# q and k of batches 1 to 3 loaded in 32-column halves and transposed by VectorE in 32x32 blocks

## The chip, the cores and the metric

The kernel runs on one core of a Trainium2 chip. TensorE (PE) multiplies matrices and writes PSUM, VectorE (DVE) and ScalarE (ACT) do elementwise work, GpSimd (POOL) does casts and issues DMAs, SyncE (SP) issues DMAs; each engine works through its own instructions in order, and semaphores tie them together. Sixteen DMA engines move the data. The metric is the device time in microseconds (us); lower is better.

## The reference

Attention in which a query only sees keys of the same hash bucket, then a gated feed-forward block on its output. Four batches, 8 heads, 768 tokens, 64 columns a head; so 3072 tokens of width 512, and an inner width of 1536.

```python
q_bits = (einsum('bhsd,dk->bhsk', q, proj) > 0)        # 6 bits
k_bits = (einsum('bhsd,dk->bhsk', k, proj) > 0)
mask = q_bucket[:, :, :, None] == k_bucket[:, :, None, :]
scores = where(mask, q @ k.T / 8, -1e9)
attn = softmax(scores) @ v                              # per batch and head
x = attn, heads side by side                            # [3072, 512]
g, val = x @ w_gate, x @ w_val                          # [3072, 1536]
ffn_out = (gelu(g) * val) @ w_out
out = x + sigmoid(x @ w_res) * ffn_out
```

## The kernel before

The work is cut into 16 pairs of heads, pair n being heads 2j and 2j+1 of batch b, n = 4b + j.

*Loading.* `load_pair(n)` (lines 75 to 81) fetches q, k and v of a pair as float32 tiles qs, ks, vs of 128 partitions by 2 heads by 6 by 64. Partition p holds tokens 6p to 6p+5, so one run in DRAM is 6 x 64 x 4 = 1536 B. Each of the three tiles has three buffers, so the load of pair n waits until pair n-3 has been read. Pairs 0 and 1 are issued on SP and ACT, all others on POOL, which also issues the weights (lines 140 to 151).

*Preparing.* `prep_pair(n)` (line 160) makes the pair's operand `aug`, 71 rows by 1536 columns for each head: 64 rows of q and k transposed and scaled (columns 0 to 767 q, 768 to 1535 k), and 7 rows of sign bits, by which the matmul of scores gives equal buckets a large bonus. It is a generator; each call of next() emits one step:
- steps 1 to 3: four PE transposes of 128x128 float32 each into a PSUM tile `tps` (line 170), and a copy to `trT` by ACT (line 174) or, for the second group of pairs from 2 on, by DVE (line 172);
- step 4: eight hash matmuls into two PSUM tiles `hps` (line 195), the signs `bits` by DVE (line 180), four small DMAs on SP that put them into rows 64 to 70 of `aug` (line 185), and the first half of the scaled copy to `aug` by DVE (line 187);
- step 5: the second half of that copy.

The tiles tps, hps and those of the feed-forward (gps, vps, rps, ops) take turns in the same three PSUM buffers (`mm_psum`).

*The main loop* (line 386) has 192 steps, 24 (`LB`) for each half batch of queries and 6 for each pair in it. A step emits two score matmuls (`sc`, line 238) and their exponential on ACT (`e`, line 241), then, two steps behind, six matmuls of attention times v (`av`, line 258), then a step of a preparation if one is due, then pieces of the feed-forward of the previous half batch: `vps` (value matmuls, line 300, with the product `gh` on DVE, line 303), `rps` and `ops` (lines 308 and 315, with `y` and `o` on DVE and the output DMA on SP, line 323). How many pieces a step gets is set by a fixed rate, not by time. At the end of a half batch x is transposed (`xps`) and the gate matmuls (`gps`, line 290) run in a row. The table `begin` says at which step the preparation of a pair starts: pairs 4 to 7 at steps 30, 36, 42 and 48, later ones every 12 steps. Loads are emitted at begin - 14.

`TS` (line 40) is the order of the 128-token tiles, even ones first, which follows from how two tiles share one transpose.

Of the kernel before, what the change touches and what calls it, by code (L numbers as in the profile page):

```python
# [13 lines left out]
ALU = mybir.AluOpType  # L14
# [5 lines left out]
def kernel(  # L20
# [19 lines left out]
    TS = [t for par in range(2) for t in range(par, T, 2)]  # L40
# [41 lines left out]


# [26 lines left out]
    ind = const.tile([P, 2], FP32, name="ind")  # L110
    for side in range(2):
        nc.vector.tensor_reduce(
            ind[:, side:side + 1],
            ident.rearrange("p (h s c) -> p h s c", h=2, s=2)[:, :, side, NBITS:NR],
            axis=AX.XY, op=ALU.add)
    shift = const.tile([P, 1], FP32, name="shift")
    nc.vector.tensor_scalar(shift, ind[:, 0:1], -1.5, 0.5, op0=ALU.mult, op1=ALU.add)
    nc.vector.scalar_tensor_tensor(shift, ind[:, 1:2], 0.25 * NBITS - 0.5, shift,
                                   op0=ALU.mult, op1=ALU.add)
# [40 lines left out]
    def prep_pair(n):  # L160
# [18 lines left out]
        for par in range(2):  # L179
            nc.vector.tensor_scalar(bits[:, par, :], hp[par][:, 0:CH], 0.0, shift,  # L180
                                    op0=ALU.is_gt, op1=ALU.subtract)
# [4 lines left out]
        for par in range(2):  # L186
            nc.vector.tensor_scalar_mul(  # L187
                a[0:D].rearrange("d h (s p n) -> d (h s) p n", s=2, p=2)[:, :, par, :],
                trT[par * D:(par + 1) * D, :].rearrange("d (i n) -> d i n", i=4), QKS)
            yield par == 0  # L190
    def hash_bits(hp, trT, groups):
# [6 lines left out]
    def prep_first():  # L198
# [13 lines left out]
        for hh in range(2):  # L212
# [4 lines left out]
            for side in range(2):  # L217
                row = 32 * (2 * hh + side)
                nc.vector.tensor_scalar(
                    a[D:KAUG, hh, side * S:(side + 1) * S].rearrange("r (p n) -> r p n", p=2),  # L220
                    hp[row:row + NR, :, 0:CH], 0.0, shift[row:row + NR], op0=ALU.is_gt, op1=ALU.subtract)
# [22 lines left out]
    def attend(i):  # L244
# [9 lines left out]
        for x in range(2):  # L254
            jt = 2 * jp + x
            for t in range(TC):
                o = (hh * TC + t) * DV
                nc.tensor.matmul(av[:, o:o + D + 1], e[:, x, t * P:(t + 1) * P],  # L258
                                 va[:, 2 * j + hh, TS[jt], :],
# [34 lines left out]
    def feed_forward(u):  # L294
# [10 lines left out]
        for t in range(TC):  # L305
# [8 lines left out]
            for kk in range(KF):  # L314
# [7 lines left out]
            nc.vector.scalar_tensor_tensor(o, y, 0.5, x_tok[u][:, t, :], op0=ALU.mult, op1=ALU.add)  # L322
            nc.sync.dma_start(
                out[b * S:(b + 1) * S, :].rearrange("(p t) d -> p t d", t=T)[:, TS[c * TC + t], :], o)
# [47 lines left out]
    def prepare(i):  # L372

        nonlocal prep
        if prep is None and todo and i >= begin[todo[0]]:
# [5 lines left out]
            prep = prep_pair(n)  # L381
# [4 lines left out]
    for i in range(NS + LEAD):  # L386
# [7 lines left out]
        for n in loads.pop(i, []):  # L394
            load_pair(n, nc.gpsimd)
# [53 lines left out]
```

## Time and profile before

| what | value |
|---|---|
| three timed runs | 376.73 us median (376.04 to 379.93) |
| the profiled execution | 378.85 us, of which the span is 377.0 |
| PE / DVE / ACT / POOL busy | 362.9 / 172.1 / 255.7 / 54.7 us |
| PE transposes (tps, L170), 180 instructions | 36.7 us busy, 5% of the chain |
| PE clock granted | 0.8 to 0.9 of full speed in the first 60 us, then full |
| DMA | 31.56 MB, engines 75 to 112% busy until 60 us, 6 to 37% after |

Busy times of lines overlap, since matmuls are pipelined: what an instruction adds to PE's time is its share of the chain, or the distance of its start from the next one's. In the chain each piece is followed back from the last instruction to what released it. "Idle before, releaser" in a group of instructions says what its engine waited for.

### The profile page before, as it was taken

The page shows a single profiled execution, that of the slowest core. Times are in us where ns is not written, and L with a number is a line of the kernel's source. Part 1 is how long each engine was busy: PE and PEld are TensorE (multiplying, and loading weights), DVE is VectorE, ACT ScalarE, POOL GpSimd, SP SyncE. Part 2 cuts the span into 40 slices and gives each one's busy share as a digit, 9 for nine tenths or more (in the row PEclk, how much of TensorE's full clock was granted, in tenths as well). Part 3 has the DMA queues.
Part 4 walks back from the last instruction along what each step waited for, and adds up shares of the span by engine and source line. Part 5 has one row for each costly group of instructions (what it writes and reads, how often), then busy time and mean ns, then how long its engine had stood idle before and what let it go on. Part 6 is the DMA issues. An engine that isn't in the chain of part 4 may idle for free.

```text
span 377.0 us, 7850 instructions
## 1 busy us (share of the span) xinstructions
PE 362.9 (96%) x3215; PEld 222.7 (59%) x3238; DVE 172.1 (46%) x305; ACT 255.7 (68%) x373; POOL 54.7 (15%) x77
## 2 busy tenths in 40 slices
PE   8788999999999999999999999999999999999995
PEld 4455666665665656665666656756566556655652
DVE  3664115667275362554346352553625242534252
ACT  5568787666866768676786768766687778686410
POOL 0973312330033200303003100000000000000000
PEclk9788699999999999999999999999999999999999
DMA  7799960444033140124103010000100010000002
GB/s 246 239 222 210 257 278 24 144 142 164 7 130 132 46 169 2 41 98 150 61 1 130 31 34 28 2 6 29 63 2 0 30 50 7 2 30 29 30 1 83
DMA packets 14140, 31.56 MB, mean 84 GB/s; under 512 B 1972, under 2 KB 6648, under 8 KB 14104
## 3 DMA queue, kind: packets, MB, share of 16 engines
q0 software_dynamic: 7984, 21.76, 20.4%
q1 hardware_dynamic: 5816, 9.10, 6.7%
q8 instruction: 25, 0.41, 0.4%
q10 hardware_dynamic: 304, 0.20, 0.2%
q14 instruction: 11, 0.09, 0.1%
HBM read 29.36 MB, written 6.29 MB: 95 GB/s over the span
## 4 chain that ended last, share of the span: by engine, by line
PE 89%; issue 3%; DVE 3%; DMA 3%; ACT 1%; POOL 0%; SPq 0%; POOLq 0%; DVEq 0%; ACTq 0%
PE gps L290 17%; PE ops L315 16%; PE vps L300 16%; PE sc L238 16%; PE av L258 9%; PE rps L308 5%; PE tps L170 5%; PE hps L195 4%; PE xps L280 2%; DMA ks<-in_k_dram 1%; DMA aug<-bits 1%; DVE aug L187 1%; DVE bits L180 1%; ACT e L241 0%; DVE gh L303 0%
## 5 line engine op out<-in xcount | busy, mean ns | idle before, releaser
L241 ACT ACTIVATE e<-sc 128x768 bf16<-128x768 f32 x192 | 152.6, 811 | 66.5 <-PE sc L238 65.5
L238 PE MATMUL sc<-aug 71*128 71x384 bf16 x384 | 96.3, 335 | 2.3 <-ACT trT L174 0.8
L303 DVE TENSOR_TENSOR gh<-vps,gh 128x384 bf16<-128x384 f32 x96 | 52.7, 555 | 91.2 <-PE vps L300 70.3
L300 PE MATMUL vps<-xT,wv 128*128 128x384 bf16 x384 | 75.2, 326 | 0.0
L258 PEld LDWEIGHTS <-e 128*128 128x128 bf16 x1152 | 58.2, 100 | 25.9 <-issue 5.3
L315 PE MATMUL ops<-wo,gh 128*128 128x512 bf16 x282 | 70.5, 379 | 0.8 <-issue 0.8
L258 PE MATMUL av<-vaug,e 128*128 128x65 bf16 x1152 | 63.4, 197 | 1.7 <-DVE xtok L268 1.7
L290 PE MATMUL gps<-xT,wg 128*128 128x384 bf16 x384 | 64.3, 326 | 0.4 <-ACT xT L283 0.4
L238 PEld LDWEIGHTS <-aug 71*128 71x128 bf16 x384 | 36.9, 100 | 33.4 <-issue 4.6
L290 PEld LDWEIGHTS <-wg 128*128 128x128 bf16 x384 | 37.6, 98 | 26.6 <-issue 0.9
L292 ACT ACTIVATE gh<-gps 128x384 bf16<-128x384 f32 x96 | 45.4, 491 | 11.3 <-PE gps L290 10.2
L300 PEld LDWEIGHTS <-wv 128*128 128x128 bf16 x384 | 34.0, 98 | 20.0 <-issue 3.7
L315 PEld LDWEIGHTS <-gh 128*128 128x128 bf16 x288 | 25.4, 98 | 24.3 <-issue 3.1
L320 DVE SCALAR_TENSOR_TENSOR y<-th,ops 128x512 f32<-128x512 bf16 x24 | 16.4, 685 | 43.6 <-PE ops L315 39.2
L187 DVE TENSOR_SCALAR aug<-trT 64x1536 bf16<-64x1536 f32 x30 | 30.0, 1000 | 0.4
L80 POOL DMA_DIRECT2D qs<-in_q_dram x14 | 10.3, 734 | 131.8 <-PE tps L170 126.4
L180 DVE TENSOR_SCALAR bits<-hps,shift 128x384 bf16<-128x384 f32 x30 | 17.1, 613 | 26.5 <-PE hps L195 26.5
L311 ACT ACTIVATE th<-rps 128x512 bf16<-128x512 f32 x24 | 14.3, 597 | 17.4 <-PE rps L308 17.4
L308 PE MATMUL rps<-wr,xT 128*128 128x512 bf16 x79 | 22.4, 379 | 1.0
L174 ACT COPY trT<-tps 128x512 f32<-128x512 f32 x31 | 17.8, 582 | 2.5 <-PE tps L170 2.5
L170 PE MATMUL tps<-ident,qs 128*128 128x128 f32 x90 | 18.5, 290 | 0.7 <-DMA qs<-in_q_dram 0.7
L170 PE MATMUL tps<-ident,ks 128*128 128x128 f32 x90 | 18.2, 287 | 0.9 <-DMA ks<-in_k_dram 0.9
(48 smaller groups left out, 211.8 us busy)
## 6 DMA issues: line engine op xcount, KB each, us to landing
out_dram<-o SPq DMA_DIRECT2D x24, 256.0 KB
qs<-in_q_dram POOLq DMA_DIRECT2D x14, 384.0 KB, 3.5
ks<-in_k_dram POOLq DMA_DIRECT2D x14, 384.0 KB, 4.7
vs<-in_v_dram POOLq DMA_DIRECT2D x14, 384.0 KB, 5.3
wg<-in_moe_w_gate_dram POOLq DMA_DIRECT2D x4, 384.0 KB, 8.2
wv<-in_moe_w_val_dram POOLq DMA_DIRECT2D x4, 384.0 KB, 12.8
wo<-in_moe_w_out_dram POOLq DMA_DIRECT2D x4, 384.0 KB, 15.6
aug<-bits SPq DMA_DIRECT2D x60, 10.5 KB
```

The lines of the kernel that those rows point to most:

```text
L170: nc.tensor.transpose(ps[:, i * P:(i + 1) * P], tiles[4 * g + i], ident)
L180: nc.vector.tensor_scalar(bits[:, par, :], hp[par][:, 0:CH], 0.0, shift, op0=ALU.is_gt, op1=ALU.subtract)
L187: nc.vector.tensor_scalar_mul(a[0:D].rearrange("d h (s p n) -> d (h s) p n", s=2, p=2)[:, :, par, :], trT[par * D:(par + 1) * D, :].rearra ...
L238: nc.tensor.matmul(sp[:, x, 0:CH], a[:, S + jt * P:S + (jt + 1) * P], a[:, c * CH:(c + 1) * CH], start=True, stop=True)
L241: nc.scalar.activation(e, sp[:, :, 0:CH], AF.Exp, scale=EXPS)
L258: nc.tensor.matmul(av[:, o:o + D + 1], e[:, x, t * P:(t + 1) * P], va[:, 2 * j + hh, TS[jt], :], start=(first and x == 0 and t == 0), stop ...
L290: nc.tensor.matmul(ps[:, 0:CH], wg[:, kk, m * P:(m + 1) * P], xT[u][:, kk, :], start=(kk == 0), stop=(kk == KM - 1))
L292: nc.scalar.activation(gh[u][:, m, :], ps[:, 0:CH], AF.Gelu)
L300: nc.tensor.matmul(ps[:, 0:CH], wv[:, kk, m * P:(m + 1) * P], xT[u][:, kk, :], start=(kk == 0), stop=(kk == KM - 1))
L303: nc.vector.tensor_mul(sl, ps[:, 0:CH], sl)
L308: nc.tensor.matmul(rps, xT[u][:, kk, t * P:(t + 1) * P], wr[:, kk, :], start=(kk == 0), stop=(kk == KM - 1))
L315: nc.tensor.matmul(ops, gh[u][:, kk, t * P:(t + 1) * P], wo[:, kk, :], start=(kk == 0), stop=(kk == KF - 1))
```

## The change

For batches 1 to 3 (pairs 4 to 15) loading and preparing are written anew; pairs 0 to 3 stay.

`load_blocks(n)` brings q and k in a layout in which transposing 32x32 blocks is all that is needed. Token 32m + p goes to partition p of a quadrant of 32 partitions; the quadrant is chosen by head and by half of the 64 columns. One tile takes four DMAs of 32 partitions by 24 by 32 float32, and a run in DRAM is 32 x 4 = 128 B. v comes with token 128t + p on partition p, in runs of 256 B. All nine DMAs of a pair are issued on SP in place of POOL.

`prep_blocks(n)` transposes with two DVE instructions, one for q and one for k, each 128 by 768 float32 from SBUF to SBUF. The result has head hh on partitions 64hh to 64hh+63. Steps: 1 transpose of q, 2 transpose of k, 3 hash matmuls, signs and their DMAs, 4 and 5 the scaled copies, one a head. The sign constant has other signs per row now, and so a second one is made at the start. Token order is natural in batches 1 to 3, which changes `TS` and the addresses of the output rows there.

```diff
+    def load_blocks(n):
+        b, j = pairs[n]
+        for nm, src in (("q", q), ("k", k)):
+            s = stage.tile([P, S // Q, Q], FP32, tag=nm + "s", name=nm + "s")
+            for hh in range(2):
+                for c in range(D // Q):
+                    g = hh * D + c * Q
+                    nc.sync.dma_start(
+                        s[g:g + Q],
+                        src[b, 2 * j + hh, :, c * Q:(c + 1) * Q].rearrange("(m p) d -> p m d", p=Q))
+            staged[(nm, n)] = s
+        s = stage.tile([P, 2, T, D], FP32, tag="vs", name="vs")
+        nc.sync.dma_start(s, v[b, 2 * j:2 * j + 2].rearrange("h (t p) d -> p h t d", p=P))
+        staged[("v", n)] = s
...
+    def prep_blocks(n):
+        b, j = pairs[n]
+        trT = tr_pool.tile([P, 2, S], FP32, tag="trT", name="trT")
+        for side, nm in enumerate("qk"):
+            nc.vector.transpose(trT[:, side, :], staged.pop((nm, n)).rearrange("p m d -> p (m d)"))
+            yield True
+        hp = [mm_psum.tile([P, 512], FP32, tag="mm", name="hps") for _ in range(2)]
+        for i in range(4):
+            for hh in range(2):
+                nc.tensor.matmul(hp[hh][32 * i:32 * i + 32, 0:CH], proj_pair[hh * D:(hh + 1) * D, :],
+                                 trT[hh * D:(hh + 1) * D, i // 2, (i % 2) * CH:(i % 2 + 1) * CH],
+                                 start=True, stop=True)
+        bits = s_pool.tile([P, 2, CH], BF16, tag="bits", name="bits")
+        for hh in range(2):
+            nc.vector.tensor_scalar(bits[:, hh, :], hp[hh][:, 0:CH], 0.0, shifts[1],
+                                    op0=ALU.is_gt, op1=ALU.subtract)
+        a = aug_of(b, j)
+        for i in range(4):
+            nc.sync.dma_start(a[D:KAUG, :, i * CH:(i + 1) * CH], bits[32 * i:32 * i + NR])
+        yield True
+        for hh in range(2):
+            nc.vector.tensor_scalar_mul(a[0:D, hh, :], trT[hh * D:(hh + 1) * D].rearrange("d s n -> d (s n)"), QKS)
+            yield hh == 0
...
-            prep = prep_pair(n)
+            prep = prep_pair(n) if n <= 3 else prep_blocks(n)
...
-            load_pair(n, nc.gpsimd)
+            load_blocks(n)
```

On DVE, the preparation of pair 4 stands among the feed-forward products `gh` of the first half batch (aug_134 before and aug_140 now is the operand of pair 4; rec and xtok belong to the attention). Before:

```order
L267 RECIPROCAL rec<-av 128x6
L268 TENSOR_TENSOR xtok<-av,rec 128x2x3x64
L303 TENSOR_TENSOR gh<-vps,gh 128x384
L172 COPY trT<-tps 128x512
L303 TENSOR_TENSOR gh<-vps,gh 128x384 x2
L180 TENSOR_SCALAR bits<-hps,shift 128x384 x2
L187 TENSOR_SCALAR aug_134<-trT 64x4x384
L303 TENSOR_TENSOR gh<-vps,gh 128x384
L187 TENSOR_SCALAR aug_134<-trT 64x4x384
```

And now:

```order
L314 RECIPROCAL rec<-av 128x6
L315 TENSOR_TENSOR xtok<-av,rec 128x2x3x64
L218 STREAM_TRANSPOSE trT<-qs 128x768
L350 TENSOR_TENSOR gh<-vps,gh 128x384
L218 STREAM_TRANSPOSE trT<-ks 128x768
L350 TENSOR_TENSOR gh<-vps,gh 128x384
L228 TENSOR_SCALAR bits<-hps,shift_131 128x384 x2
L350 TENSOR_TENSOR gh<-vps,gh 128x384
L235 TENSOR_SCALAR aug_140<-trT 64x1536
L350 TENSOR_TENSOR gh<-vps,gh 128x384
L235 TENSOR_SCALAR aug_140<-trT 64x1536
```

One copy from PSUM is gone and two transposes from the loaded tiles have come, each ahead of a product; the bits stand one step earlier, and a product lies between them and the first scaled copy.

On SP, the queue held only the bits and the outputs once the first pairs were loaded. Before, from the bits of pair 3 (aug3) to the bits of pair 6:

```order
L185 DMA aug3_133<-bits_422 7x768 x4
L185 DMA aug4_134<-bits_921 7x768 x4
L185 DMA aug5_135<-bits_1060 7x768 x4
L323 DMA out_0_dram<-o_1090 128x512
L185 DMA aug6_136<-bits_1204 7x768 x4
```

And now, from the bits of pair 3 to the bits of pair 4 (the next rows are the load of pair 7, the bits of pair 5, an output, the load of pair 8):

```order
L207 DMA aug3_139<-bits_428 7x768 x4
L93 DMA qs_518<-in_q_dram 32x24x32 x4
L93 DMA ks_523<-in_k_dram 32x24x32 x4
L98 DMA vs_528<-in_v_dram 128x12x64
L93 DMA qs_600<-in_q_dram 32x24x32 x4
L93 DMA ks_605<-in_k_dram 32x24x32 x4
L98 DMA vs_610<-in_v_dram 128x12x64
L93 DMA qs_790<-in_q_dram 32x24x32 x4
L93 DMA ks_795<-in_k_dram 32x24x32 x4
L98 DMA vs_800<-in_v_dram 128x12x64
L232 DMA aug4_140<-bits_906 7x2x384 x4
```

The loads of pairs 4, 5 and 6 stand in a row between the bits of pair 3 and those of pair 4. On POOL the same loads stood behind the weights.

35 lines of the change are left out of this document (20 added, 15 removed).

## The prediction

> **What bounds the kernel now.** I read the page first (busy shares, then the chain), then the busy time by windows, then the chain in order of time around one prepared pair, then the groups by line, and last the DMA queues and the issue times. The page's busy line and chain, and two windows of 40 us from the middle of the run (the second column is PE):
>
> ```profile
> span 377.0 us, 7850 instructions
> PE 362.9 (96%) x3215; PEld 222.7 (59%) x3238; DVE 172.1 (46%) x305; ACT 255.7 (68%) x373; POOL 54.7 (15%) x77
> ...
> PE 89%; issue 3%; DVE 3%; DMA 3%; ACT 1%; POOL 0%; SPq 0%; POOLq 0%; DVEq 0%; ACTq 0%
> PE gps L290 17%; PE ops L315 16%; PE vps L300 16%; PE sc L238 16%; PE av L258 9%; PE rps L308 5%; PE tps L170 5%; PE hps L195 4%; PE xps L280 2%; DMA ks<-in_k_dram 1%; DMA aug<-bits 1%; DVE aug L187 1%; DVE bits L180 1%; ACT e L241 0%; DVE gh L303 0%
> ```
>
> ```profile
> 100.00:140.00 40.00, 39.74 (x391) 24.81 (x393) 24.32 (x42) 27.61 (x39) 9.02 (x12) 1.00 0.32 107
> 220.00:260.00 40.00, 39.90 (x363) 25.05 (x363) 19.96 (x36) 29.44 (x43) 0.00 (x0) 1.00 0.07 23
> ```
>
> PE is the bound, and in the middle it is so without a gap: 39.74 and 39.90 of 40 us. A busy PE need not be a PE at its peak, but the chain agrees: 89% of the span is PE following PE. So whatever leaves PE's queue there shortens the run by its pitch, as long as nothing that takes its place comes late. DVE (24.32 and 19.96 of 40) and ACT (27.61 and 29.44) have room. The transposes of this change (tps, L170) hold 5% of the chain.
>
> **What leaves PE.** Their pitch is read from the chain in order of time, not from the 270 ns that one lasts, because they overlap. Pair 9's preparation (start us, us, what):
>
> ```profile
> 152.38 0.65 PE vps L300 x4
> 153.03 0.33 PE sc L238 x2
> 153.36 0.44 PE tps L170 x4
> 153.80 0.65 PE vps L300 x4
> ...
> 155.14 0.47 PE tps L170 x4
> 155.61 0.65 PE vps L300 x4
> 156.26 0.33 PE sc L238 x2
> 156.59 0.19 PE av L258 x6
> 156.78 0.47 PE tps L170 x4
> 157.24 0.65 PE vps L300 x4
> 157.89 0.33 PE sc L238 x2
> 158.22 0.18 PE av L258 x6
> 158.40 0.81 PE hps L195 x16
> ```
>
> One pair gives PE 0.44 + 0.47 + 0.47 = 1.38 us of transposes. Pairs 4 to 15 lose them, 12 x 1.38 = **16.6 us**. (Check: 5% of 377.0 us for all 15 pairs of L170 is 18.9 us; twelve fifteenths of it are 15.1.) The hash matmuls (hps) stay, in the same number and shape. Pairs 0 to 3 keep the old way.
>
> **What DVE and ACT lose and get.** The groups concerned:
>
> ```profile
> L187 DVE TENSOR_SCALAR aug<-trT 64x1536 bf16<-64x1536 f32 x30 | 30.0, 1000 | 0.4
> L180 DVE TENSOR_SCALAR bits<-hps,shift 128x384 bf16<-128x384 f32 x30 | 17.1, 613 | 26.5 <-PE hps L195 26.5
> L303 DVE TENSOR_TENSOR gh<-vps,gh 128x384 bf16<-128x384 f32 x96 | 52.7, 555 | 91.2 <-PE vps L300 70.3 <-ACT e L241 14.5 <-ACT trT L174 4.7
> L322 DVE SCALAR_TENSOR_TENSOR o<-y,xtok 128x512 f32<-128x512 f32 x24 | 16.6, 692 | 0.8
> L172 DVE COPY trT<-tps 128x512 f32<-128x512 f32 x14 | 9.7, 691 | 15.7 <-PE tps L170 15.6
> L174 ACT COPY trT<-tps 128x512 f32<-128x512 f32 x31 | 17.8, 582 | 2.5 <-PE tps L170 2.5
> L241 ACT ACTIVATE e<-sc 128x768 bf16<-128x768 f32 x192 | 152.6, 811 | 66.5 <-PE sc L238 65.5
> ```
>
> ACT loses 24 copies of L174, 24 x 0.582 = 14.0 us; nothing waits for ACT on the chain beyond 1%, so this is worth nothing by itself. DVE loses 12 copies of L172, 8.3 us. It gets 24 block transposes of 128x768 float32, which no row shows. From 384 to 512 elements DVE's time goes from 555 (L303) to 692 ns (L322), 1.07 ns an element; 768 elements come to 692 + 256 x 1.07 = **966 ns**. From below the bound is 691 ns (the 512-element copy), from above 1.93 us (966 doubled, if four-byte blocks went at half that pace). I take 966, since both rows move 32-bit data or read it at one element a time. 24 x 0.966 = 23.2 us, net 23.2 - 8.3 = +14.9 us, DVE 172.1 to 187 us: still half of the span.
>
> Whether this reaches PE is decided where DVE is fullest, in the stretches where each step also has a vps group whose product (L303) DVE must take before its PSUM buffer, one of three, is free. There a step of PE is 0.65 + 0.33 + 0.19 = 1.17 us, and a pair's five steps with the hash 5 x 1.17 + 0.81 = 6.7 us. DVE has in them 2 x 0.966 + 2 x 0.613 + 2 x 1.000 + 5 x 0.555 = 7.9 us. It falls 1.2 us behind, and has the seven steps after in which to catch up (12 steps a pair; 6 in batch 1). Three buffers bear a lag of about two steps, 2.3 us, so I charge little: the hash matmul now waits for a DVE transpose that was queued one step earlier, some 0.1 us a pair, 12 x 0.1 = 1.2 us. The PSUM buffer that three tps groups took from the same three is free now, which works the other way. The ends are 0 and, if all 1.2 us of the lag came through on all pairs, 14 us.
>
> Some steps have no feed-forward piece. There PE's step shrinks to 0.33 + 0.19 = 0.52 us, below the 811 ns of its exponential on ACT (L241); where a transpose filled such a step, up to 0.81 - 0.52 = 0.29 us of its pitch comes back. One such step a pair is 12 x 0.29 = 3.5 us at most; two score buffers let ACT run behind, and I take 0.3 us for all.
>
> The five small DVE instructions for the second sign constant come at the start, where DVE is idle until the first transposes of PE are done; nothing. The scaling to aug keeps its 64x1536 shape, about 1000 ns twice; nothing.
>
> **The loads.** This is the disputed cost. Rows of q and k are now fetched as runs of 128 B (32 float32) and v as runs of 256 B; the old loads had runs of 1536 B. One pair has 2 x 2 x 768 x 2 = 6144 runs of 128 B and 1536 of 256 B: 384 and 96 for each of the 16 DMA engines. The trace has short packets only at the start, the two proj loads (24 B runs, on q10), and long ones of 2048 B where only outputs move. Queue shares from 4.0 to 4.5 us, and from 280 to 330 us (packets, MB, share of 16 engines):
>
> ```profile
> q1 hardware_dynamic: 92, 0.12, 100.4%
> q10 hardware_dynamic: 65, 0.00, 7.3%
> ```
>
> ```profile
> DMA packets 436, 0.85 MB, mean 17 GB/s; under 512 B 48, under 2 KB 48, under 8 KB 432
> ...
> q1 hardware_dynamic: 432, 0.79, 4.1%
> ```
>
> The 24-B packet: 0.073 x 16 x 500 ns / 65 = 9.0 ns. The 2048-B one: 0.041 x 16 x 50 us = 32.8 us, less the 48 short completion packets at 9 ns, over 384 = 84 ns. On the line between them 128 B take 9.0 + 104 x 0.0372 = **12.9 ns**, and 256 B 17.6 ns. A pair then takes 384 x 12.9 + 96 x 17.6 ns = 6.6 us of all engines. The ends are 9 ns (4.3 us a pair) and 84 ns (40 us a pair); 128 B is far nearer to 24 than to 2048, but the row does not show that many short packets follow one another at this pace, and this is where my doubt lies.
>
> When must they be there? DVE meets the block transposes where PE met the old ones: it is an in-order queue, so a late load holds up the L303 products behind it, and PE one or two steps later. First transposes of pairs 4, 5, 6 and 7 (timeline of PE), and what occupies the DMA before (last weight issue on POOL, its time to landing, the last bits of pair 3 on SP):
>
> ```profile
> 59.90 0.53 PE L170 MATMUL tps<-ident,qs 128*128 128x128 f32 x3
> ...
> 69.16 0.52 PE L170 MATMUL tps<-ident,qs 128*128 128x128 f32 x3
> ...
> 78.26 0.52 PE L170 MATMUL tps<-ident,qs 128*128 128x128 f32 x3
> ...
> 99.35 0.49 PE L170 MATMUL tps<-ident,qs 128*128 128x128 f32 x3
> ```
>
> ```profile
> 30.43 0.78 POOL L148 DMA_DIRECT2D wo<-in_moe_w_out_dram  x1 [1.04 <-DMA wv<-in_moe_w_val_dram]
> ```
>
> ```profile
> DMA to landing us min/median/max: 15.3/15.6/15.9
> ```
>
> ```profile
> 30.05 2.90 SPq L185 DMA_DIRECT2D aug<-bits  x4
> ```
>
> SP's queue now holds the loads of pairs 4, 5 and 6 right behind the bits of pair 3, so they start at 33 us, beside the weights, which land by 30.4 + 15.6 = 46.0. Counting nothing before that, pair 4's q and k are there at 46.0 + 5.0 = 51.0 (wanted at 59.9), pair 5's at 57.6 (wanted at 69.2 - 1.4 = 67.8), pair 6's at 64.2 (wanted at 78.3 - 2.8 = 75.5). Later pairs come every 12 steps, some 20 us, for 6.6 us of transfer. Hidden, with 9 to 11 us to spare. SP issues nine instructions a pair; at 2.90 / 4 = 0.72 us each that is 6.5 us, for three pairs until 33 + 19.6 = 52.6, which lies beside the transfers. Behind these loads on SP stand the bits of pair 4 and, later, the outputs. Pair 4's bits come two steps after its first transpose, about when pair 6's load ends, and its scores are due at step 48, 18 steps after its preparation begins (begin[4] = 30); nothing waits there. POOL loses its load issues and keeps the casts of v; nobody else waits for it.
>
> A run's price may rise to (75.5 - 46.0) / (3 x 384 + 2 x 96) = 22 ns before pair 6 is late, and each ns more costs 1.34 us.
>
> The Trainium skill, page "DMA: Bandwidth & Descriptors", section Specifications, says that a transfer needs at least 512 B for line rate and that below it the engine does a read-modify-write. The 9.0 ns of the 24-B packets show no such cost, and the sum goes by the row; by the page it would go as the first or second rival below.
>
> **The sum.** Profiled execution: 377.0 us span, 378.85 us in all. -16.6 (PE) + 1.2 (DVE) + 0.3 (ACT) = -15.1: 363.7. The median of the three timed runs is 376.73, 2.1 lower; the same difference there gives **361.6 us**, and I say 362. Its own ends: without the two charges 360, with 3.5 from ACT and a few us of DVE lag 367.
>
> **The rivals.**
> *Short runs have a floor.* If a run under 512 B costs what 512 B cost on the line above, 9.0 + 488 x 0.0372 = 27 ns, a pair takes 480 x 27 = 13.0 us; pair 5 lands at 46.0 + 26 - 2.6 = 69.4, 1.6 late, pair 6 at 82.4, 6.9 late, the rest in time. 361.6 + 6.9 = 369. For it: no row of many short packets. Against: 9.0 ns. It is the mildest form of the page's rule. Chance 0.10.
> *The DMA engines become the bound (slower).* If each run is read and written again, 54 ns, a pair takes 26 us where the pairs come every 20; twelve take 313 us from 46, and the last pair's q and k land at about 354. The old transposes end at
>
> ```profile
> L170 PE MATMUL tps<-ident,ks x90: 270/273/476, 9.0 to 261.2; 128*128 128x128 f32 x90
> ```
>
> so the last pair is wanted near 261.2 - 16.6 = 245, and the end moves by 109 us, to 471. The gain is gone at 22 + 15.1 / 1.34 = 33 ns. In the profile it would be DVE waiting for ks and PE for DVE. Chance of above 36 ns, over 380 us: 0.13; of 30 to 36, within 1%: 0.07.
> *DVE becomes the bound.* At 1.93 us a transpose a pair's five steps give DVE 9.8 us against 6.7; in the half of the pairs that lie in vps stretches some 1.5 us of it would come through buffers, with what it holds up some 8 us in all: 370. For it: no row of this operation. Against: DVE's share. Chance 0.07.
> That the transposes don't leave PE is not open: the order of its instructions has none for pairs 4 to 15.
>
> **The numbers.** Forecast 0.63, between 358 and 367. With the floor (0.10) and DVE (0.07) the time stays under 373, faster by more than 1% (about what a measurement here can tell from no change): 0.80. Within 1% 0.07, slower 0.13. The range takes in the first three cases, 357.5 to 373, and leaves out the DMA-bound one.
>
> **What would show it.** Right: no tps of pairs 4 to 15 in the chain; windows from 100 to 260 with PE still above 39.5 of 40 us; the block transpose near 0.97 us; no wait of DVE or PE for qs or ks after 50 us; the load of a pair landing within 10 us of its issue once the weights are in. Wrong: DVE idle before the transposes with qs or ks as the releaser, the DMA share near 1 past 100 us, or hps waiting for trT by more than 0.2 us. The first two would speak for the run's price, the third for DVE.

## The result, and the profile after

The changed kernel takes **365.56 us** (median of 4 runs, 362.87 to 366.97) where the kernel before takes 376.88 us (4 runs, 376.04 to 379.93): a ratio of 0.968, with a 95% interval of 0.960 to 0.976. The forecast was 362.0 us in a range of 357.5 to 373. The profiled execution of the changed kernel is 364.91 us, its span 362.8 us; that of before was 378.85 and 377.0. So the spans lie 14.2 us apart, where the sum said 15.1.

The page of the changed kernel: span, busy times of the engines, and the chain of waits by engine and by line.

```profile
span 362.8 us, 7661 instructions
...
PE 350.9 (97%) x3094; PEld 207.2 (57%) x3094; DVE 184.1 (51%) x321; ACT 244.6 (67%) x349; POOL 27.9 (8%) x41
...
PE 92%; issue 3%; DMA 3%; ACT 1%; DVE 1%; POOL 1%; SPq 0%; POOLq 0%; DVEq 0%; ACTq 0%
PE sc L285 18%; PE vps L347 17%; PE gps L337 17%; PE ops L362 17%; PE av L305 10%; PE rps L355 6%; PE hps L223 4%; PE xps L327 2%; DMA aug<-bits 1%; DMA ks<-in_k_dram 1%; PE tps L192 1%; ACT e L288 0%; PE hps L242 0%; POOL qs L82 0%; ACT xT L330 0%
```

The transposes (tps) have fallen from 5% of the chain to 1%, which is pairs 0 to 3. PE is the bound more than before. The busy time by windows (PE, PEld, DVE, ACT, POOL, then granted clock, DMA share and GB/s) shows it, and also one stretch where DVE is now nearly full:

```profile
60.00:72.00 12.00, 11.93 (x124) 6.37 (x121) 10.74 (x19) 7.45 (x10) 1.66 (x2) 1.00 0.96 130
140.00:180.00 40.00, 40.00 (x377) 23.86 (x375) 22.95 (x39) 28.85 (x41) 1.66 (x2) 1.00 0.48 78
```

From 140 to 180 us PE has no gap at all, nor has it from there to 340. From 60 to 72 us DVE works 10.74 of 12 us. The groups by line give what DVE and PE's weight load got (count | busy us, mean ns of one | idle before, releasers):

```profile
L218 DVE STREAM_TRANSPOSE trT<-qs 128x768 f32<-128x768 f32 x12 | 11.6, 969 | 0.0
L218 DVE STREAM_TRANSPOSE trT<-ks 128x768 f32<-128x768 f32 x12 | 11.4, 947 | 0.0
L223 PEld LDWEIGHTS hps<-trT,proj_pair 64*32 64x32 f32 x192 | 3.3, 105 | 3.3 <-DVE trT L218 2.3 <-DVE gh L350 0.2
```

A block transpose takes 947 to 969 ns, waits for no load (0.0), and the hash matmuls now wait for it by 2.3 us in all.

**Where the time went.** Every half batch begins with the transposes of x (xps), so the distance of one xps group from the next is the length of a half batch. PE's timeline of the kernel before, then of the changed one, gives the first three (start us, duration us):

```profile
42.82 1.57 PE L280 MATMUL xps<-ident_bf,xtok 128*128 128x128 bf16 x12
89.66 0.83 PE L280 MATMUL xps<-ident_bf,xtok 128*128 128x128 bf16 x12
135.88 0.83 PE L280 MATMUL xps<-ident_bf,xtok 128*128 128x128 bf16 x12
```

```profile
42.62 1.57 PE L327 MATMUL xps<-ident_bf,xtok 128*128 128x128 bf16 x12
87.22 0.83 PE L327 MATMUL xps<-ident_bf,xtok 128*128 128x128 bf16 x12
130.17 0.83 PE L327 MATMUL xps<-ident_bf,xtok 128*128 128x128 bf16 x12
```

So the stretch from the first group to the second is 89.66 - 42.82 = 46.84 us before and 44.60 after. Read in this way for all (H1 holds the preparation of pairs 4 to 6, H2 of 7 to 9, H3 to H5 of two each; the rest has none):

| kernel | start of H1 | H1 | H2 | H3 | H4 | H5 | rest to the end |
|---|---|---|---|---|---|---|---|
| before | 42.82 | 46.84 | 46.22 | 43.87 | 43.93 | 43.86 | 109.46 |
| changed | 42.62 | 44.60 | 42.95 | 40.94 | 40.94 | 40.94 | 109.81 |
| difference | -0.20 | -2.24 | -3.27 | -2.93 | -2.99 | -2.92 | +0.35 |

H1 to H5 give -14.35 us, all of the gain. H1, with three pairs, gains least. The start of H1 follows the clock granted in the first 40 us, which differs between executions of one kernel (0.81 of full speed here, and 0.78 in the profile of the next run, in which H1 starts at 44.68 us); the columns behind it hardly do, and so the experiments are read by these columns.

### The profile page after: what moved, and what is told of

It is laid out like the page before. It is cut to its first block, busy times and chain, and to the rows that moved or that the text cites. A ratio compares the mean times of both kernels' runs of the same rounds, so it can differ in the third digit from the quotient of the medians.

```text
span 362.8 us, 7661 instructions
## 1 busy us (share of the span) xinstructions
PE 350.9 (97%) x3094; PEld 207.2 (57%) x3094; DVE 184.1 (51%) x321; ACT 244.6 (67%) x349; POOL 27.9 (8%) x41
## 4 chain that ended last, share of the span: by engine, by line
PE 92%; issue 3%; DMA 3%; ACT 1%; DVE 1%; POOL 1%; SPq 0%; POOLq 0%; DVEq 0%; ACTq 0%
PE sc L285 18%; PE vps L347 17%; PE gps L337 17%; PE ops L362 17%; PE av L305 10%; PE rps L355 6%; PE hps L223 4%; PE xps L327 2%; DMA aug<-bits 1%; DMA ks<-in_k_dram 1%; PE tps L192 1%; ACT e L288 0%; PE hps L242 0%; POOL qs L82 0%; ACT xT L330 0%
## 5 line engine op out<-in xcount | busy, mean ns | idle before, releaser
L285 PE MATMUL sc<-aug 71*128 71x384 bf16 x384 | 97.6, 340 | 1.5 <-DMA aug<-bits 1.1
L305 PEld LDWEIGHTS <-e 128*128 128x128 bf16 x1152 | 59.6, 101 | 25.2 <-issue 4.4
L362 PE MATMUL ops<-wo,gh 128*128 128x512 bf16 x288 | 71.9, 379 | 0.0
L180 POOL CAST vaug<-vs 128x768 bf16<-128x768 f32 x16 | 13.3, 830 | 192.1 <-DMA vs<-in_v_dram 98.9
L355 PE MATMUL rps<-wr,xT 128*128 128x512 bf16 x96 | 24.7, 380 | 0.0
L235 DVE TENSOR_SCALAR aug<-trT 64x1536 bf16<-64x1536 f32 x24 | 23.4, 976 | 0.3
L228 DVE TENSOR_SCALAR bits<-hps,shift 128x384 bf16<-128x384 f32 x24 | 13.7, 613 | 13.6 <-PE hps L223 13.6
L315 DVE TENSOR_TENSOR xtok<-av,rec 128x384 bf16<-128x384 f32 x32 | 17.8, 558 | 1.1
L369 DVE SCALAR_TENSOR_TENSOR o<-y,xtok 128x512 f32<-128x512 f32 x24 | 16.6, 692 | 0.8
L330 ACT COPY xT<-xps 128x768 bf16<-128x768 bf16 x8 | 6.4, 798 | 12.5 <-PE xps L327 12.5
```

Source lines behind the costliest of these rows:

```text
L235: nc.vector.tensor_scalar_mul(a[0:D, hh, :], trT[hh * D:(hh + 1) * D].rearrange("d s n -> d (s n)"), QKS)
L285: nc.tensor.matmul(sp[:, x, 0:CH], a[:, S + jt * P:S + (jt + 1) * P], a[:, c * CH:(c + 1) * CH], start=True, stop=True)
L315: nc.vector.tensor_mul(x_tok[u][:, :, j * P:(j + 1) * P].rearrange("p t (h d) -> p h t d", h=2), o[:, :, :, 0:D], rec.to_broadcast([P, 2, ...
L355: nc.tensor.matmul(rps, xT[u][:, kk, t * P:(t + 1) * P], wr[:, kk, :], start=(kk == 0), stop=(kk == KM - 1))
L362: nc.tensor.matmul(ops, gh[u][:, kk, t * P:(t + 1) * P], wo[:, kk, :], start=(kk == 0), stop=(kk == KF - 1))
```

## The experiments

The questions: is it the leaving of PE that pays, and how much; what gives a part of it back in H1 and H2; and do the short runs cost anything, and how near is the point at which they do. All times of half batches are read as above.

### The changed kernel once more

No edit.

> The changed kernel once more, on the same chip as scale_act and against the same runs of the kernel before. Its half batches after the first 43 us repeat within 0.2 us (44.6, 42.9, 40.9); the time of the first half batch follows the granted clock and differs from run to run by up to 5 us, which is what spreads the runs. The ratio to the kernel before should lie between 0.960 and 0.976.

Measured: 364.67 us (6 runs, 361.43 to 366.97), ratio 0.968 [0.962, 0.975]. H1 to H5 are 44.60, 42.95, 40.94, 40.94 and 40.93, each within 0.01 us of the first profile, while H1 starts at 44.68 in place of 42.62 us. So a tenth of a microsecond in a half batch means something, and two microseconds in a span need not.

### PE's transposes gone and nothing in their place

On the kernel before; pairs 4 to 15 read a constant tile in place of transposed q and k, and the copies out of PSUM that followed the transposes are gone with them:

```diff
+    still = const.tile([P, 2 * S], FP32, name="still")
+    nc.gpsimd.memset(still, 0.01)
...
+        if n <= 3:
+            trT = tr_pool.tile([P, 2 * S], FP32, tag="trT", name="trT")
+        else:
+            trT = still
...
         for g in range(3):
+            if n > 3:
+                yield True
+                continue
```

> The kernel before without the PE transposes of pairs 4 to 15 and without the copies out of PSUM that follow them; hash and scaling read a constant tile, so the transposition is what is left out. Loads stay as before. It measures the gain by itself. Theory A: PE's pitch of 16.6 us (1.38 a pair) up to 17.6 us (1.47 a pair, as the last half batches of the changed kernel give) comes off the span of 377.0 us: 359.4 to 360.4. Rival: part of the transposes filled gaps of PE, which then show; less than 14 us.

Measured: 362.30 us (4 runs), ratio 0.959 [0.952, 0.966]; the xps groups on PE's timeline:

```profile
43.17 1.41 PE L288 MATMUL xps<-ident_bf,xtok 128*128 128x128 bf16 x12
85.85 0.97 PE L288 MATMUL xps<-ident_bf,xtok 128*128 128x128 bf16 x12
127.74 0.83 PE L288 MATMUL xps<-ident_bf,xtok 128*128 128x128 bf16 x12
```

H1 to H5 are 42.68, 41.89, 40.78, 40.85 and 40.77 us: 4.16, 4.33, 3.09, 3.08 and 3.09 less than before, 17.75 in all. In H3 to H5 a pair is worth 1.55 us, against 1.38 from the chain. The rest is in the chain too, at the hash matmuls of every second pair: the kernel before, in H4, then this one.

```profile
218.12 1.14 PE hps L195 x15
```

```profile
204.14 0.81 PE hps L203 x16
```

The 0.33 us are a wait of the hash for the transposed tile; PE's weight load names ACT's copy of it:

```profile
218.39 0.18 PEld L195 LDWEIGHTS hps<-trT,proj_pair 64*32 64x32 f32 x14 [0.21 <-ACT trT L174]
```

2 x 1.38 + 0.33 = 3.09 us, as measured for H3 to H5. Against this kernel the changed one lacks 1.92 us in H1, 1.06 in H2, and 0.16, 0.09 and 0.17 in H3 to H5: **3.4 us are given back**, nearly all where three pairs are prepared in a half batch.

### The block transposes on DVE, read by nobody

The same kernel, with two block transposes a pair on DVE into a tile that nothing reads:

```diff
+            unread = tr_pool.tile([P, 2 * S], FP32, tag="trT", name="unread")
...
             if n > 3:
+                if g < 2:
+                    nc.vector.transpose(unread[:, g * S:(g + 1) * S],
+                                        (qs, ks)[g].rearrange("p h t d -> p (h t d)"))
                 yield True
                 continue
```

> The kernel no_transposes with the 24 DVE transposes added at the places where hash_later has them, into a tile that nothing reads; hash and scaling still read the constant tile. Left out as there: the transposition (the blocks transposed are not the ones needed, and unread). If DVE being full is what costs in hash_later (its products, bits and copies come late), the half batches are those of hash_later: 43.1, 42.7, 40.8. If the cost is the hash matmul waiting for the transposed tile itself, they are those of no_transposes: 42.7, 41.9, 40.8. Theory A as it stands now says the second for the most part, since DVE's products have three buffers to run behind.

Measured: 362.74 us (2 runs), ratio 0.963 [0.951, 0.974]. H3 to H5 cost nothing more (40.77, 40.85, 40.77). H1 rises from 42.68 to 43.84 us and H2 from 41.89 to 42.85, though nobody waits for a transpose here. The windows of the kernel without transposes, then of this one (the third busy time is DVE):

```profile
98.00:112.00 14.00, 13.95 (x155) 8.37 (x155) 10.74 (x20) 8.96 (x12) 0.00 (x0) 1.00 0.02 5
```

```profile
98.00:112.00 14.00, 13.79 (x152) 7.78 (x150) 12.55 (x23) 8.12 (x11) 4.28 (x6) 1.00 0.45 146
```

In H2 DVE's mere load costs 0.96 us, nearly all of the changed kernel's 1.06. H1's 1.16 of 1.92 can for the most part be of another kind. On DVE's timeline one pair of scaled copies takes 3.09 us, where two take 2 x 0.976 = 1.95 in the changed kernel, and beside it POOL casts v:

```profile
70.93 3.09 DVE L199 TENSOR_SCALAR aug<-still 64x1536 bf16<-64x1536 f32 x2
```

```profile
70.64 1.60 POOL L158 CAST vaug<-vs 128x768 bf16<-128x768 f32 x2
```

In the changed kernel a single copy of the 24 takes as long as 1.62 us. So 1.2 us is only an upper bound for DVE's load in H1; the next run gives a better figure.

### The hash one step later

The hash matmuls, which read the block transposes, move from step 3 to step 4 of the preparation, together with signs, DMAs and the first scaled copy. This kernel computes all that the changed one does.

```diff
             nc.vector.transpose(trT[:, side, :], staged.pop((nm, n)).rearrange("p m d -> p (m d)"))
             yield True
+        yield True
         hp = [mm_psum.tile([P, 512], FP32, tag="mm", name="hps") for _ in range(2)]
...
             nc.sync.dma_start(a[D:KAUG, :, i * CH:(i + 1) * CH], bits[32 * i:32 * i + NR])
-        yield True
```

> The changed kernel, with the hash matmuls one step of the main loop later (together with the first scaled copy, as in the kernel before). Theory A: the changed kernel gained 14 us and not 16.6 or more because the hash matmul of k stood waiting for DVE's transpose of k in batch 1; then the half batch from 43 to 87 us gets about 1.9 us shorter (44.6 to 42.7 us between its x transposes), the next about 0.9, the later ones stay at 40.9, and the whole is 2 to 3 us faster than the changed kernel. Rival B: the missing time went to the short loads; then no half batch changes by more than 0.5 us. Rival C: it was only the clock of the first 60 us; then also no change.

What it takes away is seen in DVE's and PE's rows of the changed kernel around pair 4. DVE's timeline, with the reciprocal (rec) and the product (xtok) that end a pair's attention:

```profile
59.94 0.18 DVE L314 RECIPROCAL rec<-av 128x6 f32<-128x6 f32 x1
60.16 0.56 DVE L315 TENSOR_TENSOR xtok<-av,rec 128x384 bf16<-128x384 f32 x1
60.75 0.98 DVE L218 STREAM_TRANSPOSE trT<-qs 128x768 f32<-128x768 f32 x1
61.65 0.52 DVE L350 TENSOR_TENSOR gh<-vps,gh 128x384 bf16<-128x384 f32 x1
62.09 0.96 DVE L218 STREAM_TRANSPOSE trT<-ks 128x768 f32<-128x768 f32 x1
```

The transpose of k ends at 63.05 us. And the chain of waits of the changed kernel there and at pair 7:

```profile
62.19 0.87 PE hps L223 x8
63.06 0.04 issue
63.11 0.85 PE hps L223 x8
...
100.24 0.81 PE hps L223 x16
```

Each group of sixteen hash passes takes 0.81 us where nothing holds it (pair 7), but 0.87 + 0.04 + 0.85 = 1.76 us at pair 4, since its second half needs k: it starts at 63.11, as soon as DVE is done. At pair 8 it is 1.15 + 0.04 + 0.85 = 2.04, and the same chain has 1.71 at pair 5, 1.09 at pair 6 and 0.94 at pairs 10, 12 and 14. Above 0.81 that is 0.95 + 0.90 + 0.28 + 1.23 + 3 x 0.13 = 3.75 us, so these rows hold all of the 3.4 us given back. In the kernel with the later hash the chain has them unbroken, at 1.06 and 0.81 us:

```profile
59.04 1.06 PE hps L224 x16
67.40 0.81 PE hps L224 x16
```

Measured: 359.68 us (6 runs, 358.57 to 366.18), ratio **0.954** [0.949, 0.960]. H1 is 43.12 us, 1.48 less than in the changed kernel, H2 42.75, 0.20 less, H3 to H5 40.81, 40.88 and 40.81, 0.32 less together: 2.0 us. H1 was near what I had expected. In H2 nearly nothing of the expected 0.9 us came: DVE is the full one there, and the wait moves to other instructions. In the chain of this run, pair 8's hash follows DVE's products:

```profile
98.44 1.01 DVE gh L350 x2
...
103.85 0.53 DVE gh L350
...
104.43 0.87 PE hps L224 x14
```

What this kernel still lacks against the one without transposes is 0.44 us in H1, 0.86 in H2 and 0.10 in H3 to H5: 1.4 of the 3.4. The medians lie 5 us below those of the changed kernel; 2.0 of that are the half batches, and the rest I can't assign to the edit, since H1 starts at 38.32 us in its profile, in a stretch where the edit changes nothing and the clock granted until 40 us was 0.93 in place of 0.81.

### A scaled copy taken from DVE: to POOL, to ACT

If DVE is full, a scaled copy of about 0.96 us a pair could go elsewhere. Both on top of the later hash:

```diff
-            nc.vector.tensor_scalar_mul(a[0:D, hh, :], ...)
+            eng = nc.vector if hh == 0 else nc.gpsimd
+            eng.tensor_scalar_mul(a[0:D, hh, :], ...)
```

> The kernel of hash_later with the second scaled copy of each pair 4 to 15 on POOL in place of DVE. Theory A: what hash_later still loses against the kernel without transposes (43.12 against 42.68 us in the half batch from 43 us on, 42.75 against 41.89 in the next) is DVE being full in the stretches with a vps group in each step, 88 to 90% busy there in the changed kernel. 1.0 us less a pair brings both half batches to within 0.2 us of 42.7 and 41.9, the later ones to 40.8: 1.0 to 1.4 us faster than hash_later. POOL is nearly idle; its copy should take about 1.7 us, twice its cast of 768 elements at 0.83. Rival: POOL's copy is late or gets in DVE's way; no gain, or slower.

```diff
+            scaled = nc.vector.tensor_scalar_mul if hh == 0 else nc.scalar.mul
+            scaled(a[0:D, hh, :], ...)
```

> The kernel of hash_later with the second scaled copy of each pair 4 to 15 on ACT in place of DVE. The theory as it stands now has two parts: the hash matmul waited for the transposes (the later hash took that away), and DVE is full in the stretches with a vps group in every step (the run with unread transposes lost 1.2 and 1.0 us in the half batches from 43 us on though no one waited for a transpose). If so, 1 us less of DVE a pair brings these half batches from 43.1 and 42.7 us towards 42.7 and 41.9, the later ones stay at 40.8, and it is 0.5 to 1.3 us faster than hash_later. ACT's copy should take about 1.5 us (its 64x768 one took 0.84). Rival: ACT's exponentials come later behind it and PE waits for them; same or slower.

To POOL: 367.69 us (6 runs), ratio 0.978 [0.971, 0.985], H1 to H5 44.34, 44.52, 41.83, 41.87 and 41.82, all longer. Groups of the kernel with POOL's copy, then the same copy with the later hash alone:

```profile
L236 POOL TENSOR_SCALAR aug<-trT 64x1536 bf16<-64x1536 f32 x12 | 49.0, 4082 | 123.4 <-DVE trT L218 109.6 <-PE sc L286 13.8
L236 DVE TENSOR_SCALAR aug<-trT 64x1536 bf16<-64x1536 f32 x12 | 24.3, 2026 | 0.0
```

```profile
L235 DVE TENSOR_SCALAR aug<-trT 64x1536 bf16<-64x1536 f32 x24 | 23.0, 957 | 0.3
```

POOL needs 4082 ns, and the copy that stayed on DVE takes 2026 in place of 957: what DVE was to be spared it pays in its other copy. (The Trainium skill, page "SBUF — State Buffer", section "Who interferes with whom", says of the port pair that DVE and GpSimd share that it is an exclusive lock held for an instruction; two copies that slow each other to this extent agree with that, and no run here separates it from other causes.)

To ACT: 368.79 us (6 runs), ratio 0.980 [0.974, 0.985]. H1 and H2 are 43.08 and 42.46, hardly better than with the later hash alone, and H3 to H5 42.30, 42.31 and 42.30, 1.4 to 1.5 us worse each. The copy takes 1468 ns on ACT, in front of exponentials, and PE's scores then wait for them 12 times, 5.5 us in all. So the 14.0 us that ACT lost by the change were no room for work put between two exponentials.

### The loads in long runs

q, k and v of pairs 4 to 15 in runs of 1536 B as before; everything else as in the changed kernel.

```diff
-            for hh in range(2):
-                for c in range(D // Q):
-                    ...
+            nc.sync.dma_start(s.rearrange("p (h t c) d -> p h (t c d)", h=2, t=T),
+                              src[b, 2 * j:2 * j + 2].rearrange("h (p t) d -> p h (t d)", t=T))
...
+        nc.sync.dma_start(s, v[b, 2 * j:2 * j + 2].rearrange("h (p t) d -> p h t d", t=T))
```

> The changed kernel with q, k and v of pairs 4 to 15 fetched in runs of 1536 B, three DMAs a pair on SP, into the same tiles. The rows land in other places than the block transposes need, so what is left out is the layout, and no amount of work on any engine. Theory A: the loads are hidden; the time is that of the changed kernel within 1 us, and every half batch is the same within 0.2 us. Rival B: the short runs cost; then about 3 us faster, most of it from 43 to 130 us.

Measured: 364.34 us (4 runs), ratio 0.966 [0.956, 0.975]; H1 to H5 44.47, 42.96, 40.94, 40.94 and 40.94. The short runs cost at most 0.13 us in a half batch here. They are hidden; they are not cheap. While one pair's load fills the engines of the changed kernel, from 106.7 to 113.8 us, the queues show:

```profile
DMA packets 7847, 1.19 MB, mean 168 GB/s; under 512 B 7830, under 2 KB 7847, under 8 KB 7847
...
q1 hardware_dynamic: 7847, 1.19, 122.3%
```

So a pair takes 7.1 us, and a packet 16 x 7.1 us / 7847 = 14.5 ns of one engine. (The share is over 100% since packets overlap on an engine; their own times, added up, would give 17.7 ns, which is more than a packet costs.) By the prediction's prices the mean would be 13.8 ns, 6.6 us a pair.

### The loads issued by POOL

```diff
-                    nc.sync.dma_start(
+                    nc.gpsimd.dma_start(
...
-        nc.sync.dma_start(s, v[b, 2 * j:2 * j + 2].rearrange("h (t p) d -> p h t d", p=P))
+        nc.gpsimd.dma_start(s, v[b, 2 * j:2 * j + 2].rearrange("h (t p) d -> p h t d", p=P))
```

> The changed kernel with the nine DMAs of each pair 4 to 15 issued on POOL in place of SP; the runs stay short. If only the engines that move the data count, the same within 1 us. If POOL's time to write descriptors counts: an old load of 256 runs took it 0.72 us; in proportion a DMA of 768 runs takes 2.2 us and one of 1536 runs 4.3, 22 us a pair, where pairs come every 20 us and in batch 1 every 10. Then pair 6's load comes some 15 to 20 us late, DVE and PE wait for qs and ks, and the time is 15 to 40 us longer than the changed kernel.

Measured: 363.48 us (2 runs), ratio 0.965 [0.952, 0.977]; H1 to H5 44.41, 42.97, 40.94, 40.94 and 40.94, the same. I had thought that POOL's issue would take longer with the number of runs. It doesn't; on POOL's timeline four such DMAs, of 768 runs each, take 0.71 us each:

```profile
49.25 2.84 POOL L93 DMA_DIRECT2D qs<-in_q_dram  x4
```

### The loads of q and k made twice, in four forms

First, each DMA of q and k is issued a second time, into a tile that nobody reads:

```diff
+            s2 = stage.tile([P, S // Q, Q], FP32, tag="twice", name="twice", bufs=2)
...
-                    nc.sync.dma_start(
-                        s[g:g + Q],
+                    for to in (s, s2):
+                        nc.sync.dma_start(
+                            to[g:g + Q],
```

> The changed kernel with each DMA of q and k issued a second time into a tile that nobody reads; a pair then asks for 768 runs of 128 B and 96 of 256 B on each DMA engine, about 13.5 us at the 7.6 us that a pair's load takes in the trace of the changed kernel. Theory A (a late load holds up DVE and then PE, and nothing is lost before): pair 5's loads come just in time, pair 6's some 4 us late, pair 7's again a few us, later ones not at all; 4 to 9 us slower than the changed kernel, all of it before 130 us. Rival (the loads have far more room than reckoned): the same time. Rival (the engines are nearly full already): the later half batches also get longer and the time passes 380 us.

Measured: 378.41 us (8 runs), ratio 1.003 [0.998, 1.008]: all of the gain is gone. H1 is 51.76 us (+7.2) and H2 49.54 (+6.6), H3 to H5 unchanged (40.94, 40.93, 40.94); I had expected 4 to 9 us. From 50 to 80 us the engines are full, at 16 x 30 us / 32366 = 14.8 ns a packet, close to the pace above:

```profile
q1 hardware_dynamic: 32366, 4.46, 125.3%
```

DVE's timeline has a late k at pair 6, then a wait for an output buffer, then a late k at pair 9; the windows show PE first and the DMA share as the last number but one:

```profile
83.70 0.98 DVE L220 STREAM_TRANSPOSE trT<-ks 128x768 f32<-128x768 f32 x1 [4.40 <-DMA ks<-in_k_dram]
...
103.79 0.69 DVE L371 SCALAR_TENSOR_TENSOR o<-y,xtok 128x512 f32<-128x512 f32 x1 [7.20 <-DMA out_dram<-o]
...
135.18 0.98 DVE L220 STREAM_TRANSPOSE trT<-ks 128x768 f32<-128x768 f32 x1 [4.91 <-DMA ks<-in_k_dram]
```

```profile
75.00:85.00 10.00, 5.62 (x56) 2.96 (x58) 4.16 (x7) 4.28 (x6) 0.00 (x0) 0.88 1.07 144
95.00:105.00 10.00, 10.00 (x62) 5.91 (x61) 2.09 (x4) 8.54 (x15) 0.83 (x1) 1.00 0.89 136
115.00:125.00 10.00, 9.91 (x95) 5.29 (x92) 6.84 (x12) 6.05 (x8) 0.83 (x1) 1.00 0.55 129
125.00:135.00 10.00, 7.18 (x71) 3.86 (x70) 3.03 (x5) 5.23 (x7) 0.00 (x0) 1.00 1.17 139
```

The two late k cost PE time: 5.62 us busy of 10 at the first, 7.18 at the second. (H1 loses more than its wait of 4.40 us; the clock granted is 0.88 in that window, 0.78 in the ten us after it, and 1.00 in the changed kernel from 70 to 90 us.) The wait for the output doesn't: from 95 to 105 us PE has no gap. And the two k are late for different reasons. At pair 6 the engines are full. Before pair 9 they are at 0.55, and the chain to its k goes over SP's issues:

```profile
129.95 0.73 SPq L95
...
130.72 4.26 DMA ks<-in_k_dram
```

SP issues seventeen DMAs a pair here, most of 0.52 us, with signs and outputs between them; it starts the load of pair 9 27.4 us after the beginning of H2, and in the changed kernel 18.4 us after it.

Three runs changed who issues what. The outputs on ACT:

```diff
-            nc.sync.dma_start(
+            nc.scalar.dma_start(
                 out[b * S:(b + 1) * S, :]...
```

> The kernel of loads_twice (each DMA of q and k issued twice) with the output DMAs on ACT's queue in place of SP's. loads_twice was 13.7 us longer than the changed kernel and not 4 to 9; its trace shows DVE 7.2 us idle for an output DMA that stood behind the loads on SP, in the half batch from 94 us on. If that queue is the second cause, that half batch falls from 49.5 us to 43 to 45, while the one before keeps its 51 to 52 us, of which the late loads are the cause. If it is the DMA engines that the output shares with the loads, it stays near 49.

Measured: 415.64 us (2 runs), ratio 1.106 [1.098, 1.114]. This settles nothing: every half batch got longer, up to the last ones (42.05, 41.39 and 34.47 us in place of 38.99, 38.32 and 32.5), since exponentials now stand behind outputs on ACT's queue. Then the outputs on POOL (`nc.gpsimd` in that place), whose queue has little else:

> The doubled loads all on SP, and the outputs issued by POOL, whose queue holds only casts of v beside them. If the 7.20 us in the second half batch came from an output that stood behind loads on SP, it goes: the second half batch comes to 43 to 44 us from 49.5, and no product waits for an output. The first half batch stays near 51.8 in either case, since its k is late whoever issues the outputs. If the second loss is a late load under another name, the second half batch stays above 47.

Measured, one run: 377.29 us; the kernel before beside it 375.74. H1 is 54.04 us and H2 46.63: +9.4 and +3.7, 13.1 in all against 13.7. No product waits for an output any more, but DVE waits for k at pair 9, in H2:

```profile
133.66 0.98 DVE L220 STREAM_TRANSPOSE trT<-ks 128x768 f32<-128x768 f32 x1 [4.64 <-DMA ks<-in_k_dram]
```

46.63 lies between what I had set for either case. The k of pair 9 is as late as with the outputs on SP (4.64 us against 4.91), so it is not the wait for the output that made it so. Why H2 is 2.9 us shorter and H1 2.3 longer is not shown by this one run. Last, only the second copies go to POOL's queue, so that SP issues nine DMAs a pair as in the changed kernel and not seventeen:

```diff
-                    for to in (s, s2):
-                        nc.sync.dma_start(
+                    for to, eng in ((s, nc.sync), (s2, nc.gpsimd)):
+                        eng.dma_start(
```

> The kernel of the doubled loads again, but the second copies are issued by POOL, so that SP issues 9 DMAs a pair as in the changed kernel, and not 17 of 0.52 to 0.64 us each. The transfers themselves are the same in number and size. If the 13.7 us were the price of the DMA engines (share 1.02 to 1.12 from 42 to 90 us), pair 6's k is late as before and the first half batch with preparations stays near 51.8 us, above 49; the second falls toward 43, since outputs then stand behind few loads. If SP's issue was what ran out, both fall to 44.6 and 43.0 within 0.7 us. From pair 8 on no theory expects a difference: 40.94.

Measured, one run: 384.49 us; H1 66.48 (+21.9), H2 42.96 (as in the changed kernel). DVE's waits for k in H1, at pairs 5 and 6, are longer than with all on SP, 5.88 and 8.24 us; the second of them:

```profile
96.48 0.98 DVE L220 STREAM_TRANSPOSE trT<-ks 128x768 f32<-128x768 f32 x1 [8.24 <-DMA ks<-in_k_dram]
```

So in H1 it is the transfers that ran out, not SP's instructions: SP issues fewer and k comes later. That it is worse than with one queue fits the issue times on POOL, which starts the useless copy of pair 6's q at 61.12 us, 9 us before SP starts the wanted one at 70.36: what nobody needs goes first. That the order is the reason was not tested apart. In H2 it is the other way: with nine DMAs on SP its loss is gone, as it must be if SP's queue made it. Loads that caught up while H1 was held would give the same, and the two were not separated.

## Why the prediction was right

**PE's transposes, 16.6 us.** Right in mechanism and a little low: 17.75 us when they and their copies are taken away, 1.55 a pair in H3 to H5 where 1.38 had been read from the chain. The sum took the hash matmuls to stay as they were. In every second pair from pair 9 on they had waited 0.33 us for ACT's copy of the transposes, and that went too.

**DVE, 1.2 us: the term that was mis-sized.** The step "the hash matmul now waits for a DVE transpose that was queued one step earlier, some 0.1 us a pair" failed in H1 and H2. DVE gives back 3.4 us, of which 3.0 fall to the six pairs 4 to 9 and 0.4 to the six others. The mechanism was named, and its ends (0 and 14 us) hold the value. The prediction's own third sign of being wrong, hps waiting for trT by more than 0.2 us, came up: the hash is 0.9 to 1.2 us late at pairs 4, 5 and 8, 0.28 at pair 6, and near the forecast, 0.13, at pairs 10, 12 and 14. Two things were left out of the sum. DVE's work in a pair's steps was counted without rec and xtok, 0.18 + 0.56 = 0.74 us in the rows above; at pair 4 they stand right ahead of the two transposes. And the "seven steps after in which to catch up" don't exist for pairs 4 to 7, which come every six steps, as the text itself said in brackets. With six products and rec and xtok a pair gives DVE 2 x 0.96 + 2 x 0.613 + 2 x 0.976 + 6 x 0.555 + 0.74 = 9.2 us, and PE 6 x 1.17 + 0.81 = 7.8. There DVE isn't an engine at half its time but the one that is nearly full, 10.74 of 12 us. Of the 3.4 us the later hash took away 2.0 (1.48 + 0.20 + 0.32); the 1.4 that stayed fit DVE's load: 0.86 of them lie in H2, where the unread transposes cost 0.96.

**The block transpose, 966 ns.** 947 and 969. The rival in which DVE becomes the bound at 1.93 us is out, but at half that price DVE held up PE in stretches of two of the eight half batches.

**ACT, 0.3 us.** Nothing of it is seen. The kernel without transposes lost ACT's copies too, and 2 x 1.38 + 0.33 leaves no loss in its H3 to H5; the changed kernel lies 0.09 to 0.17 us above it there, and 0.13 of that is the hash waiting for DVE.

**The loads.** Hidden, as forecast, and so no term of the sum; long runs give the same half batches. The price was near: 14.5 ns a packet where the mean was to be 13.8, 7.1 us a pair where it was to be 6.6. The issue on SP was not. Its rows for the first k and the end of the three loads:

```profile
40.37 9.27 SPq L93 DMA_DIRECT2D ks<-in_k_dram  x4
...
64.78 0.57 SPq L98 DMA_DIRECT2D vs<-in_v_dram  x1
```

Beside the weights a DMA took SP 2.3 us and not 0.72, and the three loads were issued until 65.4 us, not until 52.6. Even so pair 6 was there in time. The DMA share of the changed kernel is 0.94 from 66.3 to 68.1 us and 0.07 from 68.2 to 68.9, so all of its load, v too, had landed by 68.2, and its first transpose starts at 78.18: 10 us to spare, where the prediction said 9 to 11. The doubled loads bear out its cliff in H1: by its working k of pair 6 is there at 46.0 + (3 x 768 + 2 x 96) x 14.8 ns = 82.9 us, and DVE took it at 83.70. H2's loss in that run, where SP's queue is on the chain, is not in the prediction. The two rivals with dearer prices, 27 and 54 ns a run, are out. The rule of the Trainium skill, page "DMA: Bandwidth & Descriptors", section Specifications, that transfers under 512 B fall short of line rate is borne out in kind (168 GB/s with full engines from 106.7 to 113.8 us, where the kernel before, with long runs, has 315 from 40 to 50 us), but not with a price that this kernel can see.

**From the profile to the median.** The sum said 363.7 us for a profiled execution, and it was 364.91, 1.2 more. That is so near in part by luck, since two errors have opposite signs: the transposes gave 1.15 us more than forecast, and DVE took 3.4 in place of 1.2. The text then took off 2.1 us, because the profiled execution of before lay that far above its median. That of after lay 0.65 below its own, so this step alone made 2.75 of the 3.6 us between 362.0 and 365.56. An execution's offset isn't a property of the kernel: it comes with the clock of the first 40 us, 0.81 in this profile and 0.78 in that of the second run, which took 366.97.

## What to carry to other kernels

Work that is taken from the engine that bounds the run pays in full only where its receiver has room in that very stretch: sum the receiver's work over one period of the densest stretch, everything it does there counted, and not over the run. When a producer moves to another engine, give its reader one step more; a whole step cost nothing here, and made a kernel that beats both, by 2.0 us in its half batches against the changed one. A load that is hidden has a distance to its cliff, and doubling it shows in one run how near that is; but it doubles the issues too, so ask of each late load whether the engines were full or the queue. And price a packet by the time in which many of them pass, not by the packets' own times, which overlap.

## What the runs showed of the hardware

Packets of 128 and 256 B between HBM and SBUF, thousands in a row, pass at 14.5 to 14.8 ns each on an engine, while their own times add up to 122 to 125% of the engines' time. POOL issues a DMA of 768 runs in 0.71 us, and one of 256 runs took it 0.72, so the number of runs doesn't show in its issue time. SP's issue of a load's DMA takes mostly 0.5 to 1.0 us when its own loads alone fill the engines (doubled loads, 50 to 70 us), and 2.3 us beside the weights that POOL issued (changed kernel, from 40.37 us): a long issue can come from other transfers. A scaled copy of 64x1536 from float32 to bf16 takes 957 ns on DVE, 1468 on ACT and 4082 on POOL, and 2026 on DVE while POOL does the other half; beside POOL's casts two of them took DVE 3.09 us in place of 1.95.
